# A linear-attention and token-mixing kernel: quadrant transposes into two banks, one eviction and one Exp a tile, merged products, and a new written-out order

## The chip, the core and the metric

The kernel runs on one core of one Trainium2 chip. A core has five engines that run their own instruction streams and wait for each other through semaphores: TensorE (matmuls; the profile calls its matmuls PE and its weight loads PEld), VectorE (DVE), ScalarE (ACT), GpSimd (POOL), and SyncE (SP), which here only starts DMA transfers. TensorE writes its results into PSUM, eight banks of 512 fp32 words in each of 128 partitions; the other data lie in SBUF.

The metric is the time of the program on the device in microseconds, the median of several runs. A profiled execution has its own time and, inside it, a span: from the first to the last instruction.

## What is computed

The inputs `r, k, v, w, a, b` have the shape (4, 8, 768, 40): batch, heads, positions, head dimension. The first part is a recurrence over the positions, for every batch and head, on a 40x40 state:

```python
y[:, :, t] = np.einsum('bhd,bhde->bhe', rt, state)
Sa = np.einsum('bhde,bhe->bhd', state, at)
state_decay = state * wt[:, :, None, :] - np.einsum('bhd,bhe->bhde', Sa, bt)
state = state_decay + np.einsum('bhd,bhe->bhde', vt, kt)
```

Its output, with the heads side by side, is `x` of shape (4, 768, 320). The second part mixes channels and positions:

```python
theta = x @ w_theta
zr, zi = x * np.cos(theta), x * np.sin(theta)
y = einsum('ts,bsd->btd', w_tok_r, zr) + einsum('ts,bsd->btd', w_tok_i, zi)
u = x + y
out = u + np.maximum(u @ w_ch, 0.0)
```

## The kernel before

**Tiles.** The 768 positions of a batch are cut into six chunks of 128, so there are 24 tiles of 128 positions x 8 heads x 40 values. A tile is padded to 64 columns a head, so that two heads fill 128 partitions after a transpose. Inside a chunk the recurrence becomes matrix products; from chunk to chunk a state goes on.

**One tile** (`prep`, `attention_scores`, `recurrence`, `readout`):

- `prep`: ScalarE takes the logarithm of `w` (L480). TensorE sums it down the positions (`cs`, L490 and L493), ScalarE takes the Exp (`ex`, L497). The decay without the position itself, `we`, comes for the first seven tiles (`EXCLUSIVE`) from a second sum on TensorE (L503) and a second Exp (L506), and after that from a VectorE addition (`sx`, L509) and a second Exp (L514). GpSimd multiplies `k`, `b` and `a` by these (L464, three products). `v` is cast to bf16 (L469, L470).
- TensorE turns `k`, `b`, `a` and `v` (`transpose_pairs`, L427: whole 128x128 transposes through a matmul with the identity) into one bank for `k` and `b` together, one for `a`, one for `v`; ScalarE or VectorE evicts each (`evac`, L430 or L433). `r`, and `v` of the first eight tiles, come in another layout and are turned eight at a time (`turn_runs`, L558, evicted at L562).
- `scores`: four products of 128x128 a head (psi, phi, lamv, lamu), contracted over 64 rows. Two matmuls, on rows 0-63 and 64-127 of the array, write two banks (L586, `mode=64`). VectorE masks the 1,024 columns (L596), or ScalarE copies them (L598) and GpSimd zeroes a triangle (L600).
- `recurrence`: TensorE makes `x0` (L627, L633), ScalarE copies it (`nx`, L639), TensorE multiplies (`nu`, L645), ScalarE evicts (L649). The state of the next chunk is a sum of products (L666). For tiles 1 to 3 the old state is added on TensorE through the identity (`join`, L661), and for later ones on VectorE (L677) with the scaling on GpSimd (L681); the state is then transposed for the read-out (`gd`, evicted at L693).
- `readout`: 16 to 20 small matmuls (L772, L779, L781) and a product on VectorE give `x` (L788).

**Mixing.** `theta` transposes two tiles of `x` (`feature_major`, L710), multiplies with `w_theta` (`mixed`, L742; the last 64 rows of the two tiles as a pair of half-height matmuls, L752), and ScalarE copies the result out of PSUM (`eth`, L807). `sines` takes the cosine and sine of three tiles at once from that copy (L827), and `product_z` multiplies them with `x` on GpSimd, `zr` and `zi` apart (L842). When a batch is complete, `mix_row` makes for each of its six tiles twelve matmuls of 320 columns (L855) into one bank; VectorE adds `x` (L862); `channels` transposes two tiles of `u`, multiplies with `w_ch`, and VectorE applies the maximum and the sum (L878) for each tile, which SP stores (L881). `mixer_weights` and `wtok_block` load and arrange the weights; the token weights are transposed at L923.

**What sets the order.** Nothing is scheduled while it runs. Each step is recorded with `plan.add`, with its engine, its reads and writes, a cost and perhaps an alternative engine. `Plan.order` then issues the steps in the order of the list `ORDER`, which stands in the file; `HOMES` gives the PSUM banks of each step that opens a result, `PICK` the steps that take their alternative, and `WARM` the places where matmuls without use keep TensorE's clock up. Four banks are used as two pairs (`ps_d`) and four singly (`ps_s`). The costs in the code have no effect on the program as it stands.

Loads go through SP's queue, five or six transfers a tile into rings of four or five tiles (`raw_w`, `raw_kb`, `raw_a`, `raw_v`, `raw_r`); weights go through GpSimd's queue.

Of the kernel before, what the change touches and what calls it, by code (L numbers as in the profile page):

```python
# [18 lines left out]
DOUBLE = 4  # L19
FROM_POOL = 4  # L20
EXCLUSIVE = 7
RUNS = 8
ORDER = [
# [126 lines left out]
class Plan:  # L150
# [32 lines left out]
    def order(self):  # L183
# [3 lines left out]
        for n in PICK:  # L187
            self.ops[n].eng, self.ops[n].fn = self.ops[n].alts[0]
# [73 lines left out]
def kernel(  # L262
# [52 lines left out]
    def paired(t):  # L315
        return t.rearrange("p (g c) d -> p g c d", c=2)
# [418 lines left out]
    def mixed(kind, q, lhs, wt, wkeys, lkey, at="tile"):  # L735
# [11 lines left out]
        if alone(q):  # L747
            return
# [267 lines left out]
```

## Time and profile before

| | |
|---|---|
| median of three runs | 204.06 us (203.38 to 204.5) |
| the profiled execution | 205.8 us, its span 204.1 us |
| mean granted TensorE clock | 0.992 |
| busy time over the span | PE 190.9, DVE 170.2, ACT 153.5, POOL 135.3 us |
| DMA | 30.81 MB in 127,011 packets, 117,632 of them under 512 B |
| last load of a tile's data | issued at 153.2, landed at 157.5 us |
| last tile stored | its store is issued at 201.4 us |

The rows of the profile's groups give the duration of one instruction (its mean) and how much of the span the group fills. Matmuls overlap, so the mean duration of a matmul (some 220 ns for 128 columns) is not what it costs; the distance between two starts is. A row of the windows gives the busy time of each engine in a stretch, with the granted clock and the mean share of the 16 DMA engines.

### The profile page before, as it was taken

What the parts mean: (1) busy time and instruction counts of PE and PEld (TensorE: products, weight loads), DVE (VectorE), ACT (ScalarE), POOL (GpSimd) and SP (SyncE); (2) the same over time, 40 slices, a digit from 0 to 9 for tenths busy, and PEclk for the clock granted to TensorE, in tenths of its full rate; (3) what the DMA queues carried; (4) which work ended last, traced back from release to release, by engine and by line L of the source; (5) the groups of instructions that cost most, each with busy time, mean ns of one, the idle gap of its engine ahead of it and who ended that gap; (6) DMA issues with size and microseconds to landing.
All of it is one profiled execution on the core that took longest, in us unless ns stands there. A gap on an engine that the chain in (4) does not pass through costs nothing.

```text
span 204.1 us, 7885 instructions
## 1 busy us (share of the span) xinstructions
PE 190.9 (94%) x3355; PEld 154.3 (76%) x3355; DVE 170.2 (83%) x267; ACT 153.5 (75%) x345; POOL 135.3 (66%) x200
## 2 busy tenths in 40 slices
PE   6699999998999999699979999999999999999993
PEld 6576778886887788578867887988898877886761
DVE  4369989999999898698886989999999988877343
ACT  3377898989999989697977678799998954784001
POOL 8428449778997998469449949675399891349100
PEclk9799999999999999999999999999999999999999
DMA  6998999997998999799999698889999110100222
GB/s 112 214 187 212 161 171 213 181 176 158 188 209 151 180 161 206 160 193 218 152 224 162 129 193 151 153 176 179 187 194 217 34 43 3 64 3 32 101 96 96
DMA packets 127011, 30.81 MB, mean 151 GB/s; under 512 B 117632, under 2 KB 126976, under 8 KB 126976
## 3 DMA queue, kind: packets, MB, share of 16 engines
q1 hardware_dynamic: 124544, 27.54, 68.1%
q0 software_dynamic: 2432, 2.77, 7.9%
q8 instruction: 26, 0.43, 0.9%
q14 instruction: 9, 0.07, 0.1%
HBM read 29.13 MB, written 3.93 MB: 162 GB/s over the span
## 4 chain that ended last, share of the span: by engine, by line
PE 71%; ACT 11%; DMA 9%; POOL 3%; DVE 3%; issue 1%; SPq 1%; POOLq 0%
PE ps_s L855 19%; PE ps_s L427 12%; PE ps_d L586 10%; DMA raw_kb<-in_b_dram 9%; PE ps_s L742 6%; PE ps_s L710 3%; PE ps_s L645 2%; PE ps_s L558 2%; PE ps_s L666 2%; PE ps_s L752 2%; ACT cs L827 2%; PE ps_s L781 2%; PE ps_s L779 2%; PE ps_s L633 2%; PE ps_s L923 1%
## 5 line engine op out<-in xcount | busy, mean ns | idle before, releaser
L464 POOL TENSOR_TENSOR kb<-raw_kb,ex 128x320 bf16<-128x320 f32 x46 | 37.1, 818 | 16.8 <-ACT ex L497 12.0
L855 PE MATMUL ps_s<-zr,wtok_r 128*128 128x320 bf16 x144 | 40.7, 299 | 1.1 <-ACT wtok_r L930 1.1
L855 PE MATMUL ps_s<-zi,wtok_i 128*128 128x320 bf16 x144 | 40.6, 299 | 0.0
L596 DVE TENSOR_TENSOR phi<-ps_d,mask_n 128x1024 bf16<-128x1024 f32 x23 | 28.0, 1216 | 4.6 <-PE ps_d L586 4.5
L596 DVE TENSOR_TENSOR lamu<-ps_d,mask_p 128x1024 bf16<-128x1024 f32 x23 | 27.9, 1217 | 2.5 <-PE ps_d L586 2.4
L596 DVE TENSOR_TENSOR psi<-ps_d,mask_p 128x1024 bf16<-128x1024 f32 x23 | 28.0, 1218 | 2.2 <-PE ps_d L586 1.7
L842 POOL TENSOR_TENSOR zi<-cs,xp 128x320 bf16<-128x320 f32 x21 | 16.3, 791 | 10.6 <-ACT cs L827 10.6
L464 POOL TENSOR_TENSOR ah<-raw_a,we 128x320 bf16<-128x320 f32 x23 | 19.9, 864 | 4.2 <-ACT we L506 1.9
L596 DVE TENSOR_TENSOR lamv<-ps_d,mask_p 128x1024 bf16<-128x1024 f32 x17 | 20.6, 1216 | 1.3 <-PE ps_d L586 1.3
L855 PEld LDWEIGHTS <-wtok_r 128*128 128x128 bf16 x144 | 14.0, 97 | 5.7 <-ACT wtok_r L930 1.2
L842 POOL TENSOR_TENSOR zr<-cs,xp 128x320 bf16<-128x320 f32 x19 | 15.4, 821 | 4.0 <-ACT cs L827 4.0
L427 PE MATMUL ps_s<-wide,kb 128*128 128x128 bf16 x192 | 15.5, 223 | 2.5 <-POOL kb L464 2.3
L586 PE MATMUL ps_d<-aT,kbT 64*128 64x128 bf16 x384 | 17.1, 221 | 0.5 <-ACT aT L430 0.5
L855 PEld LDWEIGHTS <-wtok_i 128*128 128x128 bf16 x144 | 14.1, 98 | 3.5
L681 POOL TENSOR_TENSOR gt<-sum,ex 128x320 bf16<-128x320 f32 x13 | 9.6, 736 | 10.2 <-DVE sum L677 10.1
L862 DVE TENSOR_TENSOR up<-ps_s,xp 128x320 bf16<-128x320 f32 x22 | 10.6, 486 | 6.0 <-PE ps_s L855 5.8
L562 ACT COPY rT<-ps_s 128x512 bf16<-128x512 bf16 x24 | 13.4, 599 | 2.8 <-PE ps_s L558 2.7
L427 PEld LDWEIGHTS <-kb 128*128 128x128 bf16 x192 | 11.9, 99 | 4.2 <-POOL kb L464 2.6
L430 ACT COPY kbT<-ps_s 128x512 f32<-128x512 f32 x19 | 11.2, 591 | 4.8 <-PE ps_s L427 4.5
L779 PE MATMUL ps_s<-kb,lamv 128*128 128x40 bf16 x192 | 14.8, 180 | 0.0
L586 PEld LDWEIGHTS <-kbT 64*128 64x128 bf16 x384 | 12.3, 96 | 3.2 <-issue 1.3
L781 PE MATMUL ps_s<-kb,lamu 128*128 128x40 bf16 x192 | 14.7, 179 | 0.0
(168 smaller groups left out, 597.3 us busy)
## 6 DMA issues: line engine op xcount, KB each, us to landing
raw_w<-in_w_dram SPq DMA_DIRECT2D x24, 160.0 KB, 3.9
raw_kb<-in_b_dram SPq DMA_DIRECT2D x24, 160.0 KB, 3.8
raw_kb<-in_k_dram SPq DMA_DIRECT2D x24, 160.0 KB, 4.1
raw_a<-in_a_dram SPq DMA_DIRECT2D x24, 160.0 KB, 4.0
raw_v<-in_v_dram SPq DMA_DIRECT2D x24, 160.0 KB, 3.9
raw_r<-in_r_dram SPq DMA_DIRECT2D x24, 160.0 KB, 3.6
out_dram<-oo SPq DMA_DIRECT2D x24, 160.0 KB, 1.9
wrow_i<-in_moe_w_tok_i_dram POOLq DMA_DIRECT2D x6, 192.0 KB, 6.0
```

The costliest lines, as they stand in the source:

```text
L427: nc.tensor.transpose(out=dst[:, c:c + 128], in_=pair(src, g), identity=ident)
L430: nc.scalar.copy(out=out.bitcast(FP32), in_=in_)
L464: pool = ("POOL", lambda: nc.gpsimd.tensor_tensor(out=dst, in0=in0, in1=in1, op=ALU.mult))
L562: add("ACT", "e" + nm, i + x, lambda x=x, dst=dst: nc.scalar.copy(out=dst.rearrange("p (g t q) -> p g t q", g=G, q=8), in_=ps(pr).bitcast( ...
L586: nc.tensor.matmul(t[:, q, g, :], lhsT=lhs[rows(q), g * 128:(g + 1) * 128], rhs=rhs[rows(q), g * 128:(g + 1) * 128], start=True, stop=True)
L596: add("DVE", kindm, i, lambda: nc.vector.tensor_tensor(out=flat, in0=whole(), in1=mask.to_broadcast([128, 2 * G, 128]), op=ALU.mult), 1217 ...
L742: nc.tensor.matmul(ps(pk)[:, 0:DM], lhsT=lhs[:, c * n + kt, :], rhs=wt[:, 3 * c + kt, :], start=kt == 0, stop=kt == 2, skip_group_check=n ...
L779: nc.tensor.matmul(o, lhsT=lamv[:, p, g, :], rhs=kb[:, 0, h, 0:D], start=first, stop=False, skip_group_check=True)
L781: nc.tensor.matmul(o, lhsT=lamu[:, p, g, :], rhs=kb[:, 1, h, 0:D], start=False, stop=True, skip_group_check=True)
L842: pool = ("POOL", lambda: nc.gpsimd.tensor_tensor(out=dst, in0=in0, in1=in1, op=ALU.mult))
L855: nc.tensor.matmul(ps(pk)[:, 0:DM], lhsT=wtok[nm][:, s, j * 128:(j + 1) * 128], rhs=zs[c][:, s], start=n == 0 and c == 0, stop=n == NT - 1 ...
L862: add("DVE", "uadd", q, lambda: nc.vector.tensor_tensor(out=u, in0=ps(pk)[:, 0:DM], in1=x, op=ALU.add), 488, [pk, x_key(q)], [u_key(q)], a ...
```

## The change

1. *Transposes.* `turn` makes a 128x128 transpose out of four 64x64 ones, each on its own quadrant of the array; the two row halves write to two banks. A step recorded by `turned` opens two banks, and has whole transposes into one bank as its alternative where the blocks allow it (`turn_whole`). The new program has 3,292 quadrant transposes and 59 whole ones where there were 882 whole ones. The score products are cut into the same four quadrants.
2. *One eviction and one Exp a tile.* `k`, `b`, `a` and `v` of a tile are turned into one pair of banks and evicted by one instruction into `feat`. Both sums of the logarithm are made on TensorE for every tile (the second from the columns shifted by one), into two banks, and one Exp of 656 columns evicts them. The paths with `EXCLUSIVE` and `sx` are gone.
3. *Sin from PSUM.* The copy `th` is gone; cosine and sine of two tiles (640 columns) are taken from the banks of the product with `w_theta`. `sines` now holds that product as well.
4. *Merged products.* One GpSimd product for `k` and `b`, one for `zr` and `zi`. The addition of `x`, and the maximum and sum, work on two tiles at once, and two tiles are stored by one transfer.
5. *The state.* The old state is always joined on TensorE; VectorE scales it out of PSUM. The path over GpSimd is gone.
6. *Channel products.* The last 64 rows of two tiles meet weights padded with zeros (`wth[:, 2]`, `wth[:, 3]`), at full height; the matmuls that shifted weights at the start are gone, and two more small loads take their place.
7. *Banks.* All eight banks are four pairs, and a step takes a pair or one half of one.
8. *A new plan.* `ORDER`, `HOMES`, `PICK` and `WARM` are new. Masks on ScalarE and GpSimd go from 10 to 27 of 96, warming matmuls from 45 to 72.

```diff
+    QUADS = ((0, 0), (1, 1), (0, 1), (1, 0))
+    def turn(dst, blocks):
+        for n, parts in enumerate(blocks):
+            for c, p in QUADS:
+                nc.tensor.transpose(out=dst[rows(p), c, n * 64:n * 64 + 64],
+                                    in_=parts[p][rows(c)], identity=ident[rows(c), rows(c)])
+
+    def turn_whole(dst, blocks):
+        for n, parts in enumerate(blocks):
+            nc.tensor.transpose(out=dst[:, n * 128:n * 128 + 128], in_=parts[2], identity=ident)
...
+    def turned(kind, kinde, i, blocks, skeys, dst, dkeys, at="tile", eng="ACT", part=64):
+        p = ("ps", kind, i)
+        n = len(blocks)
+        whole = n <= 8 and all(len(parts) == 3 for parts in blocks)
+        add("PE", kind, i, lambda: turn(ps(p).bitcast(BF16), blocks), reads=skeys, writes=[p],
+            at=at, new=(p, 2), alts=(("PE", lambda: turn_whole(ps(p).bitcast(BF16), blocks)),)
+            if whole else (), **quad_cost(4 * n))
...
         add("ACT", "exp", i, lambda: nc.scalar.activation(
-            out=ex.rearrange("p h x -> p (h x)"), in_=ps(pk)[:, 0:DM + 8], func=AF.Exp),
-            440, [pk], [kex], table="lnexp")
+            out=ex.rearrange("p a h x -> p a (h x)"), in_=ps(pk)[:, :, 0:DM + 8], func=AF.Exp),
+            730, [pk], [kex], table="lnexp")
...
-        for j, nm in enumerate("kb"):
-            product("kb", i, paired(kb[:, j])[:, :, :, 0:D], paired(raw_kb[s4][:, j]), invW,
-                    [("raw_" + nm, s4), kex], [("kb", j, i % NKB)], fast)
+        product("kb", i, kb[:, :, :, 0:D], raw_kb[s4],
+                ex[:, 0:1, :, 0:D].to_broadcast([128, 2, H, D]),
+                [("raw_k", s4), ("raw_b", s4), kex], [("kb", i % NKB)], fast)
...
-        tr("tkb", "ekb", (kb[:, 0], kb[:, 1]), kbT_t[i % NTR],
-           [("kb", 0, i % NKB), ("kb", 1, i % NKB)], ("kbT", i % NTR), "ACT")
-        tr("ta", "ea", (ah,), aT_t[i % NTR], [("ah", i % 3)], ("aT", i % NTR), "ACT")
+        blocks = [two(t, g) for t in (kb[:, 0], kb[:, 1], ah) for g in range(G)]
+        skeys, dkeys = [("kb", i % NKB), ("ah", i % 3)], [("feat", st)]
         if i >= RUNS:
-            tr("tv", "ev", (vb,), vT_t[i % NTR], [("v", i % NRV)], ("vT", i % NTR), "ACT")
+            blocks += [two(vb, g) for g in range(G)]
+            skeys.append(("v", i % NRV))
+            dkeys.append(("vT", st))
+        turned("tt", "et", i, blocks, skeys, feat[:, 0:len(blocks)], dkeys)
...
             for g in range(G):
-                for q in range(2):
-                    nc.tensor.matmul(t[:, q, g, :],
-                                     lhsT=lhs[rows(q), g * 128:(g + 1) * 128],
-                                     rhs=rhs[rows(q), g * 128:(g + 1) * 128],
-                                     start=True, stop=True)
+                for q, c in QUADS:
+                    nc.tensor.matmul(t[rows(c), q, g, :], lhsT=lhs[rows(q), g, rows(c)],
+                                     rhs=rhs[rows(q), g, :], start=True, stop=True,
+                                     skip_group_check=True)
...
-            by_pool = not first and i >= FROM_POOL
-            join = not first and not by_pool
+            join = not first
...
+    def sines(q):
+        n, bi, j = (q + 1) // 2, q // NCH, q % NCH
+        cs, pk = cs_t[n % NCS], ("ps", "th", q)
+        mixed("th", q, xT_t[n % NXT], wth, [("wth", c) for c in range(3)], ("xT", n % NXT))
+        wide_ = 1 if alone(q) else 2
+        for c in range(2):
+            bias = (pi2_col[:, :], 0.0)[c]
+            def go(c=c, bias=bias):
+                src = ps(pk)[:, 0:DM] if alone(q) else ps(pk)[:, :, 0:DM]
+                nc.scalar.activation(out=cs[:, c, 0] if alone(q) else cs[:, c], in_=src,
+                                     func=AF.Sin, bias=bias)
+            add("ACT", "sin", q, go, 204 + 267 * wide_, [pk], [("cs", n % NCS, c)], table="trig")
+        for t in range(wide_):
+            z, x = z_t[bi % 2], x_of(q + t)
+            x = x.rearrange("p (a d) -> p a d", a=1).to_broadcast([128, 2, DM])
+            product("z", q + t, z[:, :, j + t], cs[:, :, t], x,
+                    [("cs", n % NCS, 0), ("cs", n % NCS, 1), x_key(q + t)],
+                    [("z", bi % 2, j + t)], q + t == N - 1)
...
+            add("DVE", "uadd2", q, lambda: nc.vector.tensor_tensor(
+                out=up_t[q // 2 % 2], in0=ps(pk)[:, :, 0:DM], in1=xp_t[q // 2 % (NX // 2)],
+                op=ALU.add), 820, [pk, x_key(q), x_key(q + 1)], [u_key(q), u_key(q + 1)],
+                at="row")
...
-WARM = {21: 32, 28: 4, 30: 2, 41: 7}
+WARM = {21: (22, 0), 25: (24, 2), 28: (2, 4), 31: (4, 6), 59: (2, 2), 63: (6, 6), 68: (2, 6), 82: (4, 6), 155: (4, 0), 195: (2, 7)}
```

More of the change, by code (lines that the diff above doesn't have):

```diff
@@ L403 @@
-    doubles = [psum.tile([128, 2, 512], FP32, name=f"ps_d{i}") for i in range(DOUBLE // 2)]
-    singles = [psum.tile([128, 512], FP32, name=f"ps_s{i}") for i in range(BANKS - DOUBLE)]
+    oo_t = sb("oo", [128, 2, DM], FP32, 2)
+    cs_t = sb("cs", [128, 2, 2, DM], FP32, NCS)
+    z_t = sb("z", [128, 2, NT, DM], BF16, 2)
+    wtok = sb("wtok", [128, 2, NT, 128], BF16, NT)
+    wrow = sb("wrow", [128, 2, S], BF16, 2)
+    doubles = [psum.tile([128, 2, 512], FP32, name=f"ps_{i}") for i in range(BANKS // 2)]
@@ L421, in pair @@
         return t[:, 2 * g:2 * g + 2, :].rearrange("p a b -> p (a b)")
-    def transpose_pairs(dst, srcs):
-        for j, src in enumerate(srcs):
-            for g in range(G):
-                c = (j * G + g) * 128
-                nc.tensor.transpose(out=dst[:, c:c + 128], in_=pair(src, g), identity=ident)
-    def copy_words(out, in_):
-        nc.scalar.copy(out=out.bitcast(FP32), in_=in_)
-    def copy_halves(out, in_):
-        nc.vector.tensor_copy(out=out, in_=in_.bitcast(BF16))
-    def evac(eng, kind, i, psk, dst, n, reads=(), writes=()):
-        act = ("ACT", lambda: copy_words(dst, ps(psk)[:, 0:n // 2]))
-        dve = ("DVE", lambda: copy_halves(dst, ps(psk)[:, 0:n // 2]))
-        one, two = (act, dve) if eng == "ACT" else (dve, act)
-        add(eng, kind, i, one[1], n, [psk], writes, alts=(two,))
+    QUADS = ((0, 0), (1, 1), (0, 1), (1, 0))
@@ L577, in turn_back @@
-        evac("ACT", "eb", i, p, vb.rearrange("p h d -> p (h d)"), 512, writes=[("v", i % NRV)])
-    def scores(i, kind, kindm, lhs, rhs, keys, dst, dkey, mask):
+            dst = ps(p).bitcast(BF16)
+            for n, parts in enumerate(blocks):
+                for c, p_ in QUADS:
+                    nc.tensor.transpose(out=dst[rows(p_), c, n * 64:n * 64 + 64],
+                                        in_=parts[p_][rows(c)],
+                                        identity=ident[rows(c), rows(c)])
@@ new lines, in turn_back, with rT_of, scores @@
+        add("PE", "tb", i, go, reads=[("vT", i % NTR)], writes=[p], new=(p, 2), **quad_cost(16))
+        add("ACT", "eb", i, lambda: nc.scalar.copy(
+            out=vb.rearrange("p (g c) d -> p c g d", c=2).bitcast(FP32),
+            in_=ps(p)[:, :, 0:128].rearrange("p c (g w) -> p c g w", g=G)),
+            380, [p], [("v", i % NRV)])
+    def rT_of(i):
+        return rT_t[i // 2 % 3][:, i % 2].rearrange("p (g c) -> p g c", g=G)
+    def scores(i, kind, kindm, lhs, rhs, keys, dst, dkeys, mask):
@@ L862, in mix_row, with chunk @@
-        add("DVE", "uadd", q, lambda: nc.vector.tensor_tensor(
-            out=u, in0=ps(pk)[:, 0:DM], in1=x, op=ALU.add), 488,
-            [pk, x_key(q)], [u_key(q)], at="row")
-        if alone(q) or j % 2:
-            channels(q if alone(q) else q - 1)
+        if not alone(q) and j % 2:
+            return
+        group = (q,) if alone(q) else (q, q + 1)
+        pk, z = ("ps", "row", q), z_t[bi % 2]
+        for t in group:
+            for s in range(NT):
+                def chunk(t=t, s=s):
+                    to = ps(pk)[:, 0:DM] if alone(q) else ps(pk)[:, t - q, 0:DM]
+                    for c in range(2):
+                        nc.tensor.matmul(to, lhsT=wtok[t % NCH][:, c, s, :], rhs=z[:, c, s],
+                                         start=s == 0 and c == 0, stop=s == NT - 1 and c == 1)
+                add("PE", "row", t, chunk, 2 * mm(320), [("z", bi % 2, s), ("wtok", t % NCH)],
+                    [pk], at="row", new=(pk, 1 if alone(q) else 2) if s == 0 and t == q else None,
+                    tail=tail(320))
@@ L891, in mixer_weights @@
                     work=260 if c else 1030)
-            up, down = wide[:, 128:256], wide[:, 0:128]
-            moves = ((((up, 0), (down, 1)), 3, slice(0, 128), 3),
-                     (((up, 1), (down, 2)), 4, slice(0, 128), 4),
-                     (((down, 0),), 2, rows(1), 2))
-            for terms, slot, part, c in moves:
-                p = ("ps", "w" + key, c)
-                def go(terms=terms, p=p, dst=dst):
-                    for m, (lhs, at) in enumerate(terms):
-                        nc.tensor.matmul(ps(p)[:, 0:DM], lhsT=lhs, rhs=dst[:, at, :],
-                                         start=m == 0, stop=m == len(terms) - 1)
-                add("PE", "wo", 10 * n + c, go, len(terms) * mm(320), [(key, 0), (key, 1)], [p],
-                    new=(p, 1), tail=tail(320), at="rel")
-                copies = [(e, lambda f=f, p=p, dst=dst, slot=slot, part=part: f(
-                    out=dst[part, slot, :], in_=ps(p)[part, 0:DM]))
-                    for e, f in (("ACT", nc.scalar.copy), ("DVE", nc.vector.tensor_copy))]
-                add("ACT", "ewo", 10 * n + c, copies[0][1], 425, [p], [(key, c)], at="rel",
-                    alts=(copies[1],))
@@ new lines, in wtok_block @@
+        row = wrow[tb % 2]
+        for c, ap in enumerate((moe_w_tok_r, moe_w_tok_i)):
+            add("POOL", "wdma", 2 + tb, lambda c=c, ap=ap: nc.gpsimd.dma_start(
+                out=row[:, c], in_=ap[tb * 128:(tb + 1) * 128, :]), 580, [],
+                [("wrow", c, tb % 2)], at="rel", work=1240)
+        blocks = [cut(row[:, c, s * 128:(s + 1) * 128]) for c in range(2) for s in range(NT)]
+        turned("wt", "ewt", i, blocks, [("wrow", 0, tb % 2), ("wrow", 1, tb % 2)],
+               wtok[tb].rearrange("p c s b -> p (c s) b"), [("wtok", tb)])
@@ L981 @@
                 nc.scalar.preload_act_table_set(LN_EXP)
+        made = []
+        nc.push_inst_callback(made.append)
         if o.fn is not None:
```

503 lines of the change are left out of this document (201 added, 302 removed), and 210 rows, old and new, of tables (HOMES, ORDER, PICK).

## The prediction

> **What bounds the kernel now.** I read the page first, for the shares of the engines and the chain that ended last. TensorE leads both:
>
> ```profile
> PE 190.9 (94%) x3355; PEld 154.3 (76%) x3355; DVE 170.2 (83%) x267; ACT 153.5 (75%) x345; POOL 135.3 (66%) x200
> PE 71%; ACT 11%; DMA 9%; POOL 3%; DVE 3%; issue 1%; SPq 1%; POOLq 0%
> ```
>
> A share is a mean over stages, so the table of windows came next (time, then the busy time of PE, PEld, DVE, ACT and POOL, the granted clock, the DMA share, GB/s):
>
> ```profile
> 20.00:40.00 20.00, 19.49 (x407) 16.10 (x407) 18.63 (x26) 17.94 (x45) 13.26 (x17) 1.00 1.00 183
> 40.00:60.00 20.00, 18.62 (x395) 15.75 (x392) 19.26 (x26) 19.35 (x47) 17.18 (x24) 1.00 0.98 181
> 60.00:80.00 20.00, 19.47 (x373) 15.60 (x370) 18.71 (x27) 18.31 (x40) 18.71 (x28) 1.00 1.01 174
> 80.00:100.00 20.00, 18.23 (x331) 15.02 (x330) 16.35 (x25) 16.06 (x37) 11.99 (x17) 1.00 0.99 185
> ...
> 120.00:140.00 20.00, 20.00 (x422) 16.87 (x420) 19.52 (x29) 17.15 (x42) 14.33 (x19) 1.00 0.88 173
> 140.00:160.00 20.00, 20.00 (x389) 17.14 (x388) 19.59 (x27) 18.74 (x44) 15.33 (x22) 1.00 0.90 176
> 160.00:180.00 20.00, 20.00 (x332) 15.63 (x331) 16.35 (x26) 13.18 (x26) 9.74 (x12) 1.00 0.10 35
> ```
>
> Two stages show. From 20 to 100 us the DMA engines are full (0.98 to 1.01), with VectorE and ScalarE near 19 of 20. From 120 us on TensorE never rests; after 160 us the loads are over and it works off what has piled up.
>
> A busy PE is not a full PE, since records of pipelined matmuls overlap. So I priced its work by the distance between starts, from the timeline (start, duration, engine, line, operation, count):
>
> ```profile
> 111.71 0.30 PE L855 MATMUL ps_s<-zr,wtok_r 128*128 128x320 bf16 x1
> 111.85 0.30 PE L855 MATMUL ps_s<-zi,wtok_i 128*128 128x320 bf16 x1
> 112.08 0.31 PE L752 MATMUL ps_s<-wch,uT 64*128 64x320 bf16 x2
> 112.23 0.61 PE L586 MATMUL ps_d<-aT,kbT 64*128 64x128 bf16 x16
> 112.77 0.31 PE L855 MATMUL ps_s<-zr,wtok_r 128*128 128x320 bf16 x1
> ...
> 113.87 0.61 PE L558 MATMUL ps_s<-wide,r 128*128 128x128 bf16 x8
> 114.31 0.30 PE L855 MATMUL ps_s<-zr,wtok_r 128*128 128x320 bf16 x1
> ...
> 116.49 0.20 PE L772 MATMUL ps_s<-gd,rT 128*128 128x80 bf16 x1
> 116.52 0.18 PE L779 MATMUL ps_s<-kb,lamv 128*128 128x40 bf16 x1
> 116.55 0.18 PE L781 MATMUL ps_s<-kb,lamu 128*128 128x40 bf16 x1
> 116.57 0.18 PE L779 MATMUL ps_s<-kb,lamv 128*128 128x40 bf16 x1
> ```
>
> A 320-column matmul takes 136 ns of the array, a whole transpose 56 (eight from 113.87 to 114.31), 80 columns 35, 40 columns 25. The sixteen 64-row score matmuls take 0.54 us with the way back to full height: eight pairs at 56 ns are 0.45, so two matmuls on different halves of the array run as one, and the change of height costs 0.09 to 0.10 us. The step from 111.85 to 112.08 says the same: 0.23 where 0.136 is usual.
>
> By these prices and the counts, TensorE's work before is: 288 row products 39.1 us, 882 transposes 49.3, 384 score pairs 21.4, 768 matmuls of 40 columns 19.2, 320 of 80 columns 11.5, 120 others of 320 columns 16.3, 22 pairs of half height 3.0, the sums of the logarithms 5.7, 45 warming matmuls 2.5: 168.0 us. With 124 changes of height at 0.095 (11.8) it is 179.8 us of a span of 204.1, 24 us unfilled, nearly all of them before 110 us.
>
> **The change, part by part.**
>
> *TensorE, transposes.* The new program has 3,292 quadrant transposes (823 blocks of 128x128) and 59 whole ones. A quadrant moves 64 columns. No row shows one. The 40- and 80-column rows (25 and 35 ns) put 64 columns at 31 ns, and the score pairs show that parts of the array which do not overlap run side by side. If all four quadrants do, a block costs 31 ns; the floor is the 25 of the 40-column row, and the ceiling is four matmuls at that floor, 100 ns. I take 31, since the half-array pairs are the nearest row and they overlap fully. The sum: 823 x (56 - 31) = 20.6 us gone, between 25.5 gone and 36.2 more.
>
> [...]
>
> *TensorE, the rest.* The scores become four quadrant matmuls where there were two halves, each still 128 columns: 56 ns a group by the pair row, no change. The channel products lose their half-height pair: 144 matmuls of 320 columns against 100 and 22 pairs, 19.6 against 16.6, +3.0 us. The second sum (L503, 7 tiles) is made for all 24: +2.4. The state is always joined on TensorE (L661, 3 to 16 times): +1.8. The ten matmuls that shifted weights go: -1.4. Warming matmuls go from 45 to 72: +1.5, in the head, where TensorE waits for the first loads anyway; if that cover is gone it is 1.5 to 3. Changes of height go from 124 to 150: +2.5. Together +9.8, so TensorE's net is -10.8 us.
>
> *ScalarE* (durations of single instructions, which sum to 180 us before). The 23 theta copies go (434 ns: -10.0). Two Exps a tile (457 and about 470) become one of 656 columns; the Sin rows of 320 and 960 columns (468 and 1001) give 0.83 ns a column, so 730 ns: -4.7 over 24 tiles. The evictions of k, b, a and v become one; 256 words take 383 and 512 take 591, so 1,024 take about 1.0 us (ceiling two of 591): -7.6. Casts that go to GpSimd: -5.2. Masks go the other way, 10 to 27 at 1.04: +17.6. Two more table loads at 1.28: +2.6. The rest -1. Net about -8.
>
> *VectorE* (184 us summed). 86 masks become 69 (1217 ns): -20.7. The 17 sums L509 go: -8.2. The state's 13 additions stay, as its scaling does, in one product: none gained. Paired additions and outputs, 320 to 640 columns, bounded by one or two of 485: I take 0.82, -3.6. Products and evictions moved off: -4. Net about -36.
>
> *GpSimd* (142 us summed). 17 more selects at 1.09: +18.6. The 13 scalings L681 go: -9.6. Casts: +5.2. Four more z products and one more kb and ah: +6. Two more weight loads on its queue, 0.7 each: +1.4. The merged products (640 columns) I price at two of 818; the 640-column cast (723) is the floor and would give some 40 us back. Net about +20, of which most falls between 20 and 160 us, where it is busy 106 of 140 now.
>
> *DMA.* The loads are the same; 24 stores become 13, of the same bytes, and two small weight loads join. The packets' time, about 155 us of 16 full engines, stays: the last load (issued at 153, landed at 157.5) can come at best some 6 us sooner. SP's queue issues eleven stores fewer, and a pair's store waits for two tiles with loads queued behind it; the ring of four tiles covers that.
>
> *Waits.* All transposes of a tile now sit in two banks and one eviction: the first score waits for k, b, a and v together, about 1.0 us of eviction instead of 0.59. The next tile is prepared one tile ahead, which hides it; without that it is 0.5 us x 24 = 10 us. Sin read from PSUM holds two banks until ScalarE has read them twice, 1.6 us.
>
> *Sum.* The profiled span is 204.1 us (that execution 205.8; the median of the runs, 204.06, equals the span, so I forecast spans). TensorE -10.8. About 40% of its work, 71.5 of 179.8 us, lies between 20 and 100 us, where full DMA engines keep the next tile from coming sooner; of those 4.3 us I give half back. 204.1 - 10.8 + 2.2 = 195.5, say 196. ScalarE's and VectorE's relief is spent on keeping TensorE fed.
>
> **The rivals.**
>
> *B: a quadrant block costs as much as a whole transpose (slower).* Place: the weight load in front of each quadrant. The rows of weight loads on the page last 96 to 99 ns each and TensorE's load side is busy 76% of the span; today each load is overlapped by others, and if four quarter loads do not overlap, a block stays at 56. Then nothing is gained by transposes and 9.8 us are lost: 204.1 + 9.8 = 214. It decides from 56 - 9.8/0.823 = 44 ns a block up. [...] Against it: loads already overlap at 25 ns a matmul in the 40-column rows.
>
> *C: quadrants are bound by issue.* The fastest sustained stream is a load and a matmul in 25 ns. If that is the sequencer's pace, a block costs 100 ns (+36.2) and a score group 100 instead of 56 (+16.9): 204.1 + 53 + 9.8 = 267. Against it: two matmuls of a score pair start within 4 ns.
>
> *D: GpSimd takes TensorE's place.* Its 20 us more lie where it is already busy 94% (60 to 80 us), and 27 masks go through ScalarE and then GpSimd (1.04 + 1.09 instead of 1.22 us). If half of its 20 us shows, TensorE's gain is gone: 204. For it: ScalarE and VectorE are near full there too. Against: GpSimd waits most for ScalarE, which gets lighter.
>
> **How the numbers follow.** My case, with a block near 31 and up to 38 ns, has 0.60, and 188 to 201 of its own (floor 25 ns: 4.9 less; 38 ns: 5.8 more, rounded). B 0.17, near 214, down to 206 at half its price. C 0.11. D 0.12, 200 to 207. A measurement here tells 0.5%, 1 us, from no change. Faster: 0.60 and 0.04 of D; the same: 0.05 of D; slower: 0.17, 0.11 and 0.03: 0.31. The range, 187 to 214, takes in my case, D and most of B, and leaves out C and the upper end of B.
>
> **What would show it.** Right: quadrant transposes in groups of four, starts a few ns apart and a group about 31 ns after the last; TensorE's stream near 169 us; theta's copy gone from ScalarE; DVE's busy time near 137 and GpSimd's near 155; the last load landing before 155 us and the stretch after it shorter than 46 us. Wrong: groups 56 ns or more apart (B), or single starts 25 ns apart (C); GpSimd without a gap from 20 to 160 us with TensorE waiting for `kb`, `z` or the masks (D).

## The result, and the profile after

The changed kernel takes **250.15 us** (249.59 to 252.24, four runs) beside 204.06 us: a ratio of 1.228, with a 95% interval from 1.220 to 1.236. It is 46 us slower where 8 us less were forecast, far beyond the range that was given. The profiled execution spans 248.2 us (44.1 more than before) at a mean granted clock of 0.917. Below, each ratio is to executions of the kernel before made beside the run (medians of 204.56 to 205.12 us). Times are medians of all executions, while a ratio leaves out those over 1.5% above the fastest of their kernel, so it can differ a little from the quotient of the medians.

The page of the changed kernel: the busy time of the engines, the transfers of instructions, the granted clock, and the chain that ended last.

```profile
PE 203.5 (82%) x6639; PEld 159.0 (64%) x6639; DVE 141.2 (57%) x198; ACT 155.9 (63%) x269; POOL 147.5 (59%) x176
PEclk9999999755977889979979999997995899999999
q8 instruction: 52, 0.85, 1.4%
PE 70%; issue 14%; ACT 8%; DVE 5%; DMA 1%; POOL 1%; DVEq 0%; ACTq 0%; POOLq 0%
```

No engine is full any more: TensorE is at 82%, the others near 60%. What has grown in the chain is "issue", from 1% to 14%: time in which TensorE waited for nothing that the profile records. The instruction count has doubled, from 3,355 to 6,639 matmuls, each with its weight load. The queue that brings instructions shows 52 packets of 16 KB. In the kernel before it showed half of that:

```profile
q8 instruction: 26, 0.43, 0.9%
```

The windows of the changed kernel (time, busy time of PE, PEld, DVE, ACT and POOL, granted clock, DMA share, GB/s), the answer to those of before:

```profile
40.00:60.00 20.00, 13.90 (x528) 11.56 (x529) 10.58 (x12) 11.38 (x23) 9.87 (x11) 0.68 0.88 163
60.00:80.00 20.00, 16.58 (x511) 12.39 (x507) 14.70 (x19) 14.11 (x23) 11.37 (x14) 0.81 0.97 171
80.00:100.00 20.00, 16.36 (x623) 12.99 (x623) 12.21 (x16) 12.52 (x21) 13.12 (x14) 0.91 0.91 157
...
160.00:180.00 20.00, 14.81 (x589) 11.92 (x582) 14.00 (x17) 14.30 (x23) 10.47 (x13) 0.91 0.84 178
```

TensorE and its three feeders are all partly idle in the same stretches: from 40 to 60 us VectorE does 10.58 us of work where it did 19.26, GpSimd 9.87 where it did 17.18. So none of the feeders is what holds the others up. The timeline of TensorE (start, duration, engine, line, operation, count, idle time before and its releaser) shows how:

```profile
100.79 0.20 PE L620 MATMUL ps<-gt,feat 128*128 128x80 bf16 x1
100.82 0.20 PE L625 MATMUL ps<-v,psi 128*128 128x40 bf16 x2
103.08 0.21 PE L620 MATMUL ps<-gt,feat 128*128 128x80 bf16 x1 [2.05 <-issue]
103.12 0.21 PE L625 MATMUL ps<-v,psi 128*128 128x40 bf16 x2
```

In the middle of a row of matmuls whose data are all there, nothing runs for 2.05 us. TensorE's gaps of over 0.4 us put down to "issue", counted from the start of one matmul to the start of the next, add up to 38.2 us, and to some 42.6 with the small ones; in the kernel before there is none over 0.4. Counting loads and matmuls in the trace, all of them lie at positions 193 + 256k of TensorE's stream (705, 1217, 1473, 1729 and so on), 27 of the 52 blocks of 256. Each time TensorE goes on 1.26 to 1.63 us after one of the instruction packets has ended. Where TensorE stalls, the time from the entry into one block to the entry into the next is most often 4.00 us (7 times of 27; the others lie between 3.3 and 6.2, so the 3.9 us "at best" of the expectations below is the author's estimate). In the kernel before, no block of 256 was used up in less than 5.14 us. All this looks as if TensorE were short of instructions.

At 4.0 us each, 52 blocks are an estimated 208 us, more than the kernel before takes, whatever the matmuls cost. It is no strict bound: blocks entered without a stall follow each other after as little as 2.4 us.

### The profile page after: what moved, and what is told of

Same layout as the page of the kernel before. It is cut to its first block, busy times and chain, and to the rows that moved or that the text cites. A ratio compares the mean times of both kernels' runs of the same rounds, so it can differ in the third digit from the quotient of the medians.

```text
span 248.2 us, 14286 instructions
## 1 busy us (share of the span) xinstructions
PE 203.5 (82%) x6639; PEld 159.0 (64%) x6639; DVE 141.2 (57%) x198; ACT 155.9 (63%) x269; POOL 147.5 (59%) x176
## 4 chain that ended last, share of the span: by engine, by line
PE 70%; issue 14%; ACT 8%; DVE 5%; DMA 1%; POOL 1%; DVEq 0%; ACTq 0%; POOLq 0%
PE ps L784 17%; PE ps L406 12%; PE ps L580 11%; PE ps L706 10%; PE ps L731 4%; PE ps L657 2%; PE ps L637 2%; DVE lam L589 2%; ACT ex L506 2%; PE ps L725 2%; PE ps L495 2%; PE ps L502 2%; ACT feat L439 1%; PE ps L625 1%; PE ps L411 1%
## 5 line engine op out<-in xcount | busy, mean ns | idle before, releaser
L589 DVE TENSOR_TENSOR lam<-ps,mask_p 128x1024 bf16<-128x1024 f32 x39 | 47.3, 1220 | 19.5 <-PE ps L580 19.2
L784 PE MATMUL ps<-z,wtok 128*128 128x320 bf16 x288 | 47.2, 301 | 1.2 <-issue 1.2
L472 POOL TENSOR_TENSOR kb<-raw_kb,ex 128x640 bf16<-128x640 f32 x24 | 34.3, 1428 | 21.7 <-ACT ex L506 21.1
L472 POOL TENSOR_TENSOR z<-cs,xp 128x640 bf16<-128x640 f32 x22 | 30.4, 1398 | 18.6 <-ACT cs L763 18.6
L784 PEld LDWEIGHTS <-wtok 128*128 128x128 bf16 x288 | 25.5, 98 | 10.9 <-issue 1.5
L580 PEld LDWEIGHTS <-feat 64*64 64x64 bf16 x1152 | 21.5, 116 | 15.9 <-issue 12.0
L589 DVE TENSOR_TENSOR psi<-ps,mask_p 128x1024 bf16<-128x1024 f32 x18 | 22.0, 1221 | 14.0 <-PE ps L580 13.8
L580 PE MATMUL ps<-feat 64*64 64x128 bf16 x768 | 21.8, 239 | 7.2 <-issue 6.2
L472 POOL TENSOR_TENSOR ah<-raw_a,ex 128x320 bf16<-128x320 f32 x24 | 19.4, 807 | 13.2 <-ACT ex L506 12.1
L506 ACT ACTIVATE ex<-ps 128x656 f32<-128x656 f32 x24 | 17.3, 721 | 11.8 <-PE ps L502 11.6
L591 ACT ACTIVATE phi<-ps 128x1024 bf16<-128x1024 f32 x12 | 12.2, 1025 | 7.4 <-PE ps L580 7.4
L738 DVE TENSOR_TENSOR xp<-ps,ex 128x320 bf16<-128x320 f32 x22 | 10.6, 485 | 9.6 <-PE ps L731 9.5
L641 ACT ACTIVATE nu<-ps 128x320 bf16<-128x320 f32 x24 | 10.6, 441 | 8.7 <-PE ps L637 8.6
```

Source lines behind the costliest of these rows:

```text
L472: pool = ("POOL", lambda: nc.gpsimd.tensor_tensor(out=dst, in0=in0, in1=in1, op=ALU.mult))
L506: add("ACT", "exp", i, lambda: nc.scalar.activation(out=ex.rearrange("p a h x -> p a (h x)"), in_=ps(pk)[:, :, 0:DM + 8], func=AF.Exp), 73 ...
L580: nc.tensor.matmul(t[rows(c), q, g, :], lhsT=lhs[rows(q), g, rows(c)], rhs=rhs[rows(q), g, :], start=True, stop=True, skip_group_check=True)
L589: add("DVE", kindm, i, lambda: nc.vector.tensor_tensor(out=flat, in0=whole(), in1=mask.to_broadcast([128, 2 * G, 128]), op=ALU.mult), 1217 ...
L591: 1217, [p], dkeys, alts=(("ACT", lambda: nc.scalar.mul(out=flat, in_=whole(), mul=sign)),))
L641: add("ACT", "enu", i, lambda: nc.scalar.mul(out=nu[:, :, 0:D], in_=ps(pk)[:, 0:DM].rearrange("p (h d) -> p h d", h=H), mul=-1.0), 437, [p ...
```

## The experiments

**Theories.** T: TensorE runs dry of instructions, because a block of 256 takes about 4.0 us to come and the quadrants, two instructions each, use it up sooner. R: the new plan, its pairs of banks or its heavier GpSimd cause the loss. Q: quadrants are slow in themselves (the prediction's rivals B and C). D: the traffic of the loads delays the instructions.

**Half the instructions for the same moves.** One transpose of 64 rows to 128 columns does what two quadrants do; it writes the same two banks, and the plan, the evictions and the products stay. A few transposes (22 blocks of the fifth piece) remain quadrants.

```diff
-            for c, p in QUADS:
-                nc.tensor.transpose(out=dst[rows(p), c, n * 64:n * 64 + 64],
-                                    in_=parts[p][rows(c)], identity=ident[rows(c), rows(c)])
+            for c in range(2):
+                nc.tensor.transpose(out=dst[:, c, n * 64:n * 64 + 64],
+                                    in_=parts[2][rows(c)], identity=ident[rows(c), rows(c)])
...
-                for q, c in QUADS:
-                    nc.tensor.matmul(t[rows(c), q, g, :], lhsT=lhs[rows(q), g, rows(c)],
+                for q in range(2):
+                    nc.tensor.matmul(t[:, q, g, :], lhsT=lhs[rows(q), g, :],
```

> The changed kernel with its plan, banks, evictions and products as they are, but TensorE issues half as many instructions for the same array work: a block is turned by two 64-row, 128-column transposes into the same two banks (two matmuls in place of four), and a score group is two matmuls of 64 rows as before the change. 8,549 TensorE instructions in place of 13,289; 22 blocks whose halves lie apart stay quadrants. Theory T (TensorE runs out of instructions: they come in blocks of 256, one every 3.9 us at best, and each block used up sooner leaves it idle, 38 us in all): 34 blocks, so the idle time put down to issue falls from 38 us to under 5, the granted clock returns to 0.97 or more, and the time is 195 to 210 us. Rival R (the new plan, the pairs of banks or GpSimd's longer list hold it up, and the issue waits are their shadow): the time stays above 235 us. Rival Q (quadrants themselves are dear): the transposes' starts get closer than 31 ns a block.

Measured: 207.82 us, ratio 1.012 (1.0045 to 1.020). The page of this kernel, engines and chain:

```profile
PE 189.7 (92%) x4269; PEld 146.6 (71%) x4269; DVE 139.8 (68%) x198; ACT 154.0 (75%) x269; POOL 147.5 (72%) x176
PE 51%; DMA 13%; SPq 10%; POOL 8%; ACT 7%; DVE 6%; issue 3%; POOLq 0%; DVEq 0%
```

The time is in T's range. Some 42 of the 46 us are back, with the plan, the banks, the evictions and GpSimd's work all as in the changed kernel. R falls for all but a few of the 46 us. The gaps of "issue" over 0.4 us are 0.6 us in all. Q falls too: where nothing stalls, a block takes 31 to 32 ns as quadrants and mostly 29 as halves. The chain now runs in part through the loads and SP's queue (DMA 13%, SPq 10%), to which the last two runs come back.

**One half of it at a time.** Only the scores as halves (the second part of the diff), and only the transposes as halves (the first part):

> The changed kernel with the scores alone as two matmuls of 64 rows; the transposes stay quadrants: 11,753 TensorE instructions, 46 blocks, 77 more changes of the array's tiling than the changed kernel (227, 7 us of array time). Theory T: 6 blocks fewer to wait for, 23 us less waiting at most, 7 us given back: 230 to 245 us. Rival R: 250 to 258 us, only the 7 us more.

> The changed kernel with the transposes alone as two halves; the scores stay quadrants: 10,085 TensorE instructions, 39 blocks, 248 changes of tiling (9 us of array time more). Theory T: between the run with both and the run with the scores alone: 210 to 228 us. Rival R: 250 to 260 us.

Measured: 233.76 us, ratio 1.138 (1.1275 to 1.149), with the scores as halves; 213.09 us, ratio 1.038 (1.029 to 1.047), with the transposes as halves, both as T had said. The first leaves 11,753 instructions on TensorE and 25.8 us of "issue" gaps, the second 10,085 and 2.0 us. The second has 248 changes of the array's tiling where the kernel with both halves has 187; at 0.095 us these 61 are an estimated 5.8 us, about what it takes more (5.3 us).

**The kernel before, with more instructions and nothing else.** Its plan, banks and feeders stay; each score matmul of 64 rows and 128 columns is cut into four of 32 columns.

```diff
-                    nc.tensor.matmul(t[:, q, g, :],
-                                     lhsT=lhs[rows(q), g * 128:(g + 1) * 128],
+                    for c in range(4):
+                        nc.tensor.matmul(t[32 * c:32 * c + 32, q, g, :],
+                                         lhsT=lhs[rows(q), g * 128 + 32 * c:g * 128 + 32 * c + 32],
```

> The kernel before, its plan and everything else untouched, but each score group is eight matmuls of 64 rows by 32 columns in place of two of 64 by 128: the same 128 columns through the same array in parallel, 11,327 TensorE instructions in place of 6,719. Theory T: 44 blocks in place of 26, 44 x 3.9 = 172 us of supply, so the average still fits, but stretches rich in scores wait: 212 to 235 us, with idle time put down to issue, which the kernel before has not. Rival R (plan, banks, GpSimd): 202 to 207 us.

Measured: 231.95 us, ratio 1.130 (1.1205 to 1.139). Its page:

```profile
PE 202.2 (88%) x5659; PEld 162.3 (70%) x5659; DVE 173.3 (75%) x267; ACT 155.5 (67%) x345; POOL 135.3 (59%) x200
q8 instruction: 44, 0.72, 1.3%
PE 75%; ACT 9%; issue 9%; DVE 4%; POOL 2%; POOLq 0%
```

The loss appears in the old kernel too as soon as it has 11,327 instructions on TensorE: 22.5 us of gaps at every 256th instruction where there were none. A score group of eight starts 56 to 67 ns after the last where a pair took 56, an estimated 3 to 4 us over the 384 groups, which together with the gaps is about the 27 us that were lost. The granted clock was 0.981 here, so the loss does not need the low clock of the changed kernel. Over the six kernels the gaps follow the count of instructions, not the plan:

| kernel | instructions on TensorE | gaps over 0.4 us, "issue" or at every 256th instruction | ratio to before |
|---|---|---|---|
| before | 6,719 | none | 1 |
| all halves | 8,549 | 0.6 us | 1.012 |
| transposes as halves | 10,085 | 2.0 us | 1.038 |
| before, scores in eighths | 11,327 | 22.5 us | 1.130 |
| scores as halves | 11,753 | 25.8 us | 1.138 |
| changed | 13,289 | 38.2 us | 1.228 |

**The supply by itself.** A small kernel that is not this computation (its output is zeros): 5,120 quadrant transposes of a constant that wait for nothing, the first 2,048 with no transfer running, the others beside loads of inputs like the kernel's.

> Not the kernel's computation at all: 5,120 quadrant transposes of a constant on TensorE (10,240 instructions with their weight loads, 40 blocks of 256), the first 2,048 with no transfer running, the rest while 96 loads of 160 KB go through SP's queue; the output is zeros. By the array alone a block of 256 instructions, 32 transposed blocks, would take 1.0 us. Theory T with one block of look-ahead: 4.0 us a block, so about 64 us for the first stretch and 96 to 110 for the second, with idle time put down to issue at every 256th instruction. Rival D (the loads that fill the DMA engines hold up the instruction transfers): under 2.5 us a block in the first stretch and about 4 in the second. Rival Q (the sequencer issues one instruction every 12.5 ns): 3.2 us a block without gaps.

The timeline of this kernel, first without loads, then with them:

```profile
35.30 1.92 PE L36 MATMUL ps_a<-ident,data 64*64 64x64 bf16 x128 [1.80 <-issue]
38.75 1.92 PE L36 MATMUL ps_a<-ident,data 64*64 64x64 bf16 x128 [1.53 <-issue]
42.21 1.92 PE L36 MATMUL ps_a<-ident,data 64*64 64x64 bf16 x128 [1.53 <-issue]
...
100.98 1.93 PE L36 MATMUL ps_b<-ident,data 64*64 64x64 bf16 x128 [2.35 <-issue]
105.53 1.92 PE L36 MATMUL ps_b<-ident,data 64*64 64x64 bf16 x128 [2.62 <-issue]
109.81 1.93 PE L36 MATMUL ps_b<-ident,data 64*64 64x64 bf16 x128 [2.35 <-issue]
```

128 transposes with their 128 weight loads, a gap, and again: exactly 256 instructions at a time. The distance between starts is mostly 3.45 or 3.73 us with the DMA engines idle (a mean of 3.59) and 4.28 to 4.83 us among the loads (a mean of 4.50). The limit is there without any dependence, any plan and any other traffic, so T holds, with a block of the first stretch 0.4 us cheaper than it had said. Rivals D and Q fall as they were put: D wanted under 2.5 us a block in the first stretch, Q no gaps. The loads add some 0.9 us a block, which is the part of D that is true.

The packets of instructions in this trace show what the time consists of. In the first stretch the packet for the next block mostly starts 1.0 to 1.2 us after a block has been entered, lasts 0.9 to 1.4 us, and TensorE goes on 1.2 to 1.6 us after its end. So one block is fetched ahead and no more, and most of the time is spent before and after the transfer. Among the loads the packet mostly starts 1.7 to 2.6 us after the entry, and lasts no longer. The mean granted clock was 0.52 here, with TensorE busy 42% of the span; while the clock was still full, at 6.02 us, a block's work took 1.24 us and the next block came after 3.73 us all the same.

**The changed kernel without most of its loads.** From tile 8 on, each load of an input brings 8 of 128 rows, so those tiles are computed from stale data and the output is not the reference's. The same cut was made in two more kernels, below.

```diff
         for key, dst, src in load(i):
+            if i >= 8:
+                dst, src = dst[0:8], src[0:8]
```

> The changed kernel itself, with quadrants, and the same loads cut to 8 rows. Theory T (instruction supply; a block of 256 takes 3.45 to 3.73 us with the DMA engines idle and about 4.0 among the loads): the stalls shrink by 0.3 to 0.5 us at each of 27 blocks, 8 to 14 us, so 234 to 242 us, and gaps at every 256th instruction remain, 24 to 30 us in all. If the transfers of the inputs alone made the instructions late, the gaps would go and it would take 180 to 190 us.

Measured: 236.37 us; one execution of the four took 232.72 us, the others 236.23 to 237.33. The trace is of the slowest and has 28.3 us of "issue" gaps; the commonest time between entries into blocks where TensorE stalls falls from 4.00 to 3.73 us. T had said 234 to 242 us and 24 to 30 us of gaps; the fastest execution lies 1 us under its range, and far from the 180 to 190 us of the other case. The page of this kernel, chain:

```profile
PE 70%; issue 11%; ACT 8%; DVE 6%; POOL 2%; POOLq 0%; DVEq 0%
```

So some 10 of the 38 us of stalls go with the loads' traffic, and some 28 are there without most of it; the time is 13 to 17 us shorter.

**Where the promised gain went.** With halves everywhere TensorE does less than before, yet the kernel is not faster. First the remaining quadrants were taken out: the fifth block of a pair of tiles is cut from the two tiles laid flat, and the weights for it are loaded again, shifted, instead of padded.

```diff
-        return [cut(t[:, c, m:m + 128]) for c in range(2) for m in (0, 128)] + [
-            (t[:, 0, 256:DM], t[:, 1, 256:DM])]
+        flat = t.rearrange("p c d -> p (c d)")
+        return [cut(flat[:, m:m + 128]) for m in (0, 128, 256, 384, 512)]
```

> The run with halves, and the 22 blocks that had stayed quadrants become halves too: the five blocks of a pair of tiles are cut from the 640 columns in a row, as before the change, and the channel weights are loaded a second time, shifted by 64 rows, by two more loads on GpSimd's queue. 8,461 TensorE instructions, 150 changes of tiling in place of 187. 37 changes at 0.095 us are 3.5 us of TensorE's work. If what is left above the kernel before (207.8 against 205.1) is TensorE's work: 203 to 205.5 us. If it is waiting in the new plan, which hides 3.5 us of TensorE's work: 206 to 208 us.

Measured: 207.41 us, ratio 1.009 (1.005 to 1.013): no faster than before. That is the case of waiting: 3.5 us less work on TensorE brought 0.4 us. Then masks were put back on VectorE, where they were before, to relieve ScalarE and GpSimd: the 12 of phi, and all 27.

```diff
-            1217, [p], dkeys, alts=(("ACT", lambda: nc.scalar.mul(
+            1217, [p], dkeys, alts=() if kind == "sphi" else (("ACT", lambda: nc.scalar.mul(
```

> The run before this one in the list, with the 12 phi masks that the new plan gives to ScalarE and GpSimd back on VectorE; everything else in the plan's order. Theory P (with the instructions there, the masks' way over two engines is what TensorE waits for: 1.0 and 1.1 us in place of 1.2): 2 to 5 us faster than that run. Rival V (VectorE, busy 140 us, stands at those places in the order already): 0 to 6 us slower than that run.

> As the run before, but all 27 masks of ScalarE and GpSimd on VectorE: 33 us more work there, 28 us less on ScalarE and 29 us less on GpSimd. Theory P: 2 to 6 us faster than the run with the flat blocks. Rival V: 3 to 12 us slower.

Measured: 218.08 us, ratio 1.057 (1.048 to 1.067), and 229.69 us, ratio 1.117 (1.109 to 1.125). Each mask moved back costs 0.8 to 0.9 us, of the 1.22 that it takes VectorE. Theory P falls; rival V had the direction right and the size too small (11 and 22 us slower than the flat kernel, where at most 6 and 12 were expected). The waits of TensorE in the kernel with all 27 moved back:

```profile
PE ps L582 <- DVE phi L591: 4.8, 4, 1.8
PE ps L582 <- DVE psi L591: 2.7, 4, 1.1
PE ps L784 <- DVE up L794: 2.5, 1, 2.5
```

TensorE now waits for VectorE, although that is busy only 75% of the span. So moving masks off ScalarE and GpSimd does not help in this order. What lighter engines would bring without a heavier VectorE these two runs do not show.

Last, the loads: the same cut of all loads from tile 8 on, in the kernel before and in the flat one.

> The kernel before, with the loads of k, b, a, w, v and r from tile 8 on cut to 8 of 128 rows, so that those tiles are worked out from stale data and the output is not the reference's; nothing else changes. TensorE's work stays 179.8 us. Theory L (the transfers of the inputs hold the tiles back until 100 us, so a lighter TensorE cannot gain there): 186 to 194 us here, TensorE's waits between 20 and 100 us gone. Rival G (the other engines and the written order hold TensorE, not the loads): 199 to 205 us, waits as in the kernel before.

> The flat version of the changed kernel (halves, no quadrants) with the same loads cut to 8 rows. TensorE's work is 169.9 us. Theory L: 176 to 184 us, some 10 us under the kernel before with the same cut, so that the gain that TensorE's work promised is seen once the loads are out of the way. Rival G: no less than the kernel before with the cut, within 3 us of it, and the waits for ScalarE and GpSimd between 20 and 100 us (16.0 us with full loads) remain above 10 us.

Measured: 204.24 us for the kernel before, ratio 0.999 (0.996 to 1.0015), and 205.08 us for the flat one, ratio 1.002 (0.998 to 1.006). Rival G is what came, for both. The cut brings the DMA share to about 0.6 from 50 to 60 us and lower after that. Two windows of each, first the kernel before with the cut, then the flat one:

```profile
60.00:80.00 20.00, 19.81 (x387) 16.18 (x381) 19.07 (x29) 18.53 (x40) 19.08 (x28) 1.00 0.34 53
80.00:100.00 20.00, 20.00 (x363) 16.33 (x361) 17.95 (x28) 17.94 (x39) 13.13 (x19) 1.00 0.40 65
```

```profile
60.00:80.00 20.00, 19.34 (x492) 14.88 (x490) 17.81 (x23) 17.79 (x28) 17.91 (x20) 1.00 0.27 42
80.00:100.00 20.00, 18.60 (x510) 14.68 (x506) 14.89 (x20) 16.45 (x30) 19.42 (x24) 1.00 0.48 64
```

The DMA share was 1.01 and 0.99 in these windows of the kernel before; with a third to two fifths of it the kernel takes the same time. The loads, full as their engines were, do not set the end of the kernel before from 50 us on, and that of the flat one by some 1% at most; before that the cut changes little, and the question stays open. The flat kernel still rests in both windows. Its chain, first with all loads, then with the cut:

```profile
PE 44%; SPq 17%; DMA 14%; POOL 12%; DVE 6%; issue 4%; ACT 2%; POOLq 0%; DVEq 0%
PE 61%; ACT 13%; SPq 10%; DVE 5%; DMA 5%; POOL 3%; issue 2%; DVEq 0%; POOLq 0%
```

With all loads the chain runs through SP's queue and the loads again and again until 85 us, with the cut only until 51 us, and the time is nearly the same; so the chain here is one path among several of about the same length.

Its account against the kernel before, by the prices of the prediction and the gaps beyond them: work 153.4 (with a block at 29 ns) + 150 x 0.095 = 167.6 us (169.9 with a block at 31 ns, as in the expectations) against 179.8, waits 28.5 against 17.5. The 9.9 to 12.2 us of saved work are met by 11.0 us of new waits, most of them between 20 and 100 us (16.0 us against 7.7), in small pieces, for some fifteen different steps of ScalarE, GpSimd and VectorE; with the loads cut they are still 15.8. (Such sums of small gaps move by 2 to 5 us with the length from which a gap is counted.) Whether the written order is to blame or the longer steps themselves (one eviction of about 0.94 us, a product of 1.43, a mask by two engines) no run here separates. No version that was run beats the kernel before.

## Why the prediction was wrong, point by point

- *Quadrant transposes at 31 ns a block: right.* Four starts within about 10 ns, the next four most often 31 to 32 ns after the first; a score group 55 to 56 ns. The price came from two rows of other shapes, and it held. Rival B falls: weight loads of a quarter array last 115 to 117 ns on average in the three costliest of their rows of after, and a block with four of them still takes 31 to 32 ns, so they overlap all the same. The half transposes of the later run take 14.5 ns each, 29 a block, with half the instructions.
- *TensorE's work: right.* Forecast 169.0 us with a block at 31 ns; by the counts of after, with a block at 31.5 ns, it is 155.5 + 14.3 = 169.8.
- *The other engines: near, GpSimd too high.* The summed durations went from 180.4 to 170.2 us on ScalarE (-10.2, forecast -8), from 183.8 to 147.5 on VectorE (-36.3, forecast -36) and from 142.1 to 152.7 on GpSimd (+10.6, forecast +20: the merged products take 1.40 and 1.43 us where two of 818 ns were counted, which is 0.2 us less on each of 46).
- *The step that failed is the sum itself:* "TensorE -10.8" took the array's time for TensorE's time. It put at nothing what it takes to bring the instructions in: twice as many, 256 at a time, and about 4.0 us for each 256. The prediction knew the counts (3,292 quadrants for 882 transposes, four matmuls for two) and used them for the array only. The page of before had a row for it, 26 instruction packets. Its blocks lasted 5.14 us at the least, 1.1 us over the 4.0 that after shows, and twice the instructions for the same work would leave an estimated 2.6 us. The limit itself no row of before shows, since nothing stalled there. Of the 54 us between the forecast 196 and the measured 250, 42 go with the instructions (the run with halves takes them back); the other 12 are the gain that does not come even then (208 in place of 196).
- *Rival C was the nearest, and wrong in its mechanism.* It asked whether each instruction needs 12.5 ns to be issued (by what it calls the sequencer), found pairs 4 ns apart, and gave 267 us a chance of 0.11. In after the matmuls of a quadrant group do mostly start 3 to 4 ns apart. What fell short is the mean: 4.0 us / 256 = 15.6 ns an instruction at the commonest stalled block, by which a block of quadrant transposes with its four loads is an estimated 125 ns when nothing else is mixed in. That the loss was 44 us and not more may be due to the long matmuls of 320 columns that lie between; no run separates that.
- *The sizes.* Against before, TensorE's work is 10.0 us less, its "issue" gaps 41.9 us more (42.6 against 0.7), its other waits 4.2 us more (21.0 against 16.8): +36.1 of the 44.1 us of span. For the other 8.0 the trace offers the granted clock, 0.917 against 0.992; an estimate from it, 169.8 x (1/0.917 - 1/0.992) = 14.0 us, is of that order, but no run changed the clock alone.
- *Half of 4.3 us given back: wrong in size and in reason.* The reason, that full DMA engines keep the next tile from coming sooner, is not borne out from 50 us on. And where the instructions suffice, all of TensorE's gain is given back: 9.9 to 12.2 us of work against 11.0 us of waits. Why the waits grow stays open.
- *Rival D* said that if half of GpSimd's 20 us shows, the time is 204. The flat kernel lands at 207, but its waits are spread over three engines, and moving GpSimd's masks to VectorE makes it worse. As the one cause D is not borne out; a share in it is neither shown nor excluded.
- *Signs.* Right: groups 31 ns apart, the stream, theta's copy gone. Near: VectorE busy 141.2 us (137 forecast) and GpSimd 147.5 (155). Wrong: the last load landed at 199.4 us, not before 155, and the stretch after it lasted 48.8 us, not under 46. A pair's store held SP's queue for 35.2 us, from 97 to 132 us, the longest such wait, with loads behind it; the prediction had left that to the ring of four tiles. In the flat kernel, with the same paired stores, the longest such wait between 20 and 170 us is 6.2 us, which speaks for a consequence of the late TensorE rather than a cause.

## What to carry to other kernels

Price TensorE's program by instructions as well as by array time: a matmul with its weight load was two here (6,639 of each), and 256 of them needed 3.5 to 4.8 us to arrive, with one block fetched ahead, so a stretch in which several blocks in a row use less than that stands still. The sign in a profile is "issue" in the chain (14% here, 1% before), and gaps in the middle of ready work at every 256th instruction. When a tiling can do the same moves with fewer and wider instructions (here 64x128 instead of 64x64, 29 ns a block against 31 to 32), take it; and when an engine of a tightly ordered kernel gets lighter, ask which waits the order will put in place of its work.

## What the runs showed of the hardware

- TensorE's instructions come in packets of 16 KB, 256 of them in each: 26 packets for the 6,719 instructions of the kernel before, 52 for the 13,289 of the changed one, with the stalls at every 256th. The fetch is not hidden here: mostly 3.45 to 3.73 us a block with the DMA engines idle, of which the transfer itself is 0.9 to 1.4 us, 4.0 most often in the changed kernel where it stalls, 4.28 to 4.83 among dense loads, against 1.92 us for the work of the block at half clock.
- The granted clock was 0.52 in the small kernel, where TensorE was busy 42% of the span, 0.68 from 40 to 60 us of the changed kernel (busy 13.90 of 20 us) and 0.999 in the profile of the version with halves (busy 92%). But from 0 to 40 us of the changed kernel it was 1.00 with TensorE busy 14.52 and 15.18 of 20 us, so rest and a lower clock do not always go together. Of the warming matmuls, those at the start of the kernel before begin 107 ns apart at first and 56 ns apart from 4.08 us on; after that TensorE was busy 1.93 us of the 4 to 8 us, the granted clock was 0.5 from 7.47 to 10.89 us and matmuls of 128 columns began 107 ns apart again. No run left the warming matmuls out, so what they bring is not measured.
- Quarter-array matmuls on four different quadrants run together: a group of four score matmuls of 128 columns most often takes 55 to 56 ns, as much as one whole transpose of 128 columns in the kernel before (eight in 0.44 us, from 113.87 to 114.31).
- A DMA share of 1.00 need not be a bound: it was 1.01 and 0.99 from 60 to 100 us of the kernel before, and with the loads from tile 8 on cut to a sixteenth, the kernel before took 0.999 of its time (0.996 to 1.0015).
